# Attention, low-rank mixing and FFN on one core: the early pairs' pooled result goes into the mixing products, and four pairs are early instead of five

## The chip, the cores and the metric

The kernel runs on one core of a Trainium2 chip. The metric is the device time of one execution in microseconds. The core's engines are TensorE (PE; PEld is its weight load), VectorE (DVE), ScalarE (ACT), GpSimd (POOL) and SyncE (SP), each with its own queue of instructions that it works through in order. All DMAs of this kernel are issued by SP.

## The reference, cut to what matters

```python
def _attn_ref(q, k, v):                                # 8 batches, 8 heads, 576 positions, 64 wide
    ...                                                # q_d, k_d, v_d: means over 4 neighbours
    out_d = sm_attn(q_d, k_d, v_d)                     # 144 x 144 attention
    out_up = np.repeat(out_d, factor, axis=2)          # each pooled row four times
    mask = np.abs(pos[:, None] - pos[None, :]) < factor
    ...
    out_local = np.matmul(attn, v)                     # 7 keys around each position
    return (out_up + out_local).astype(np.float32)

def _moe_ref(x, U, V, w_ch1, w_ch2):                   # x: heads side by side, 512 wide
    xt = x.transpose(0, 2, 1)
    h = xt @ U @ V                                     # rank 32, over the positions
    u = x + h.transpose(0, 2, 1)
    ch = np.maximum(u @ w_ch1, 0.0) @ w_ch2            # 512 -> 2048 -> 512
    return (u + ch).astype(np.float32)
```

## The kernel before, in words

Work is cut into 32 pairs of heads, pair = 4 * batch + hp, and 256 FFN steps: batch, one of two halves of 288 positions, and one of 16 slices of 128 hidden channels. A step has a first layer (line 889, tile ps_h, 12 matmuls), ACT and DVE splitting its result into a high and a low part (hH, hL), and a second layer (line 913, tiles acc, 12 matmuls) three steps later. The low parts (W1L, W2L, uL, hL) exist because every FFN product is done three times, high x high, high x low and low x high.

The order on each engine is fixed when the program is built. The code lists operations with an engine, a duration, a priority, tiles read and written; `Plan.run` plays them through, gives out buffers, and writes the instructions in the order of the start times that it found. On the chip each engine follows that order, and waits when something is late.

Before the FFN of a batch can start, its four pairs must have left their mixed result u in the tiles uH and uL, one set for each half. There are two forms of a pair:

- Early form (pairs 0 to 4). The local part is a block product on PE: scores of 32 queries against 38 keys (L602) under a band mask (L613), softmax, transposes (ps_bt, L644) and the product with the values (ps_ba, L656). The pooled part is ps_v, ps_s, ps_t and ps_a (L433 to L486), with the result od. These tiles lie in a memory pool that is given back once all early operations are done; W2's tiles take its place, and the planner's operation "late" stands for that moment. Pairs 0 to 3, which are batch 0, are mixed at once by `early_mix`: hu (L678) multiplies the local result ob by U (Ublk), um (L693, L695) multiplies that (stk) by V and adds ob through the identity. Pair 4 stores its result to DRAM (x_s, L666 and L667), and `mix_part` reads it back later.
- Late form (pairs 5 to 31). Scores of both parts come from PE (L720, L727); the local product is done on POOL (Pt, L800) and DVE (acc, L805) from values vl; the result goes through DRAM (x_s) to `mix_part`: xL, xH and Y, hu (L849), u (L864), then uH on ACT and uL on POOL (L872). There is one vl buffer, and Pt has three buffers, shared with the raw weights w1r and w2r.

In the early form the pooled result reaches the sum in this way: od is stored to DRAM (up_e, L493), and read back (L588) into rows 38 to 45 of each block's value tile vw, after vw's own load:

```python
        for hh in range(2):
            dma(lambda hh=hh: nc.sync.dma_start(
                out=vw_t()[hh * KW + KL:hh * KW + KU, 0:NL],
                in_=up_s()[hh].rearrange("(n j) d -> j n d", j=QL // 4)), [(up_s, hh), (vw_t, hh)], [(vw_t, 2 + hh)], prio, 40)
```

The weight tile ms_b has a fixed pattern in the same eight columns, copied once from pat: a one where the query belongs to that pooled row. So the one product ps_ba adds both parts. vw has two tiles that take turns, so the load of a later pair waits for the ps_ba of an earlier one.

All weights come as 64-bit numbers and are converted in pieces (`convert`): a DMA of 512 KB into a raw buffer, ACT (L346), three DVE operations (L348, L350, L352), ACT for the high part (L354) and POOL for the low one (L357). W1 has 16 pieces and W2 has 16.

## Time and profile before

| | |
|---|---|
| median of 3 runs | 1029.94 us (1028.54 to 1030.81) |
| profiled execution | 1032.15 us |
| its span, first to last instruction | 1030.3 us |
| PE busy | 995.5 us, 97% of the span |
| DVE, ACT, POOL busy | 488.6, 387.3, 539.1 us |
| mean granted clock of PE | 0.978 |
| moved by DMA | 120.30 MB |

A profile is of one execution. Its page has the busy time of each engine, the span in 40 equal slices (digits are tenths), the DMA queues, the chain of work that ended last, followed back from the end, and groups of equal instructions. A row of a timeline has start, duration, engine, line, operation, out<-in, shapes, the count of merged instructions and, in brackets, the idle time of the engine before it with what ended it. One fp32 matmul of the code is two records where its operands are split. A row of waits reads "engine line <- what it waited for: us in total, times, the longest". Busy times of PE overlap, since matmuls are pipelined; the distance from start to start is what one costs in a stream.

### The profile page before, as it was taken

Reading aid. Unit: us, or ns where it says so; the run is one execution under the profiler, and the core shown is the slowest. Engines: PE = TensorE matmul, PEld = TensorE weight load, DVE = VectorE, ACT = ScalarE, POOL = GpSimd, SP = SyncE. Lnnn points to the kernel's source line nnn. Section 1 sums busy time; section 2 is a strip of 40 time slices with the busy share of each in tenths; the row PEclk is TensorE's granted clock in tenths of the full one; section 3 lists DMA queues with packets and bytes.
Section 4 is the critical chain, followed back from the end, with each engine's and each line's share of the span. In section 5 each row is a group of like instructions: output and inputs, shape, how many; then the busy total and the mean of one; then the engine's idle time right before and its main releaser. Section 6 shows DMA issues by size and latency. Waiting matters only on the chain.

```text
span 1030.3 us, 26938 instructions
## 1 busy us (share of the span) xinstructions
PE 995.5 (97%) x10831; PEld 975.6 (95%) x10831; DVE 488.6 (47%) x1018; ACT 387.3 (38%) x1234; POOL 539.1 (52%) x567
## 2 busy tenths in 40 slices
PE   6887899999999999999999999999999999999998
PEld 4666889999999999999999999999999999999998
DVE  5667676555454545445554434553454424212111
ACT  4665565344334433343533235333343232111110
POOL 4643568796755756376775527762675605211010
PEclk9787999999999999999999999999999999999999
DMA  9766874655555444556556336534465231000000
GB/s 292 228 177 181 214 191 126 148 145 131 121 143 117 122 108 100 128 136 145 134 121 137 91 81 146 139 83 113 110 144 131 75 78 35 24 1 24 2 24 24
DMA packets 222612, 120.30 MB, mean 117 GB/s; under 512 B 175492, under 2 KB 198456, under 8 KB 222488
## 3 DMA queue, kind: packets, MB, share of 16 engines
q1 hardware_dynamic: 222488, 118.58, 45.9%
q8 instruction: 85, 1.39, 0.6%
q14 instruction: 39, 0.32, 0.1%
HBM read 87.78 MB, written 30.75 MB: 115 GB/s over the span
## 4 chain that ended last, share of the span: by engine, by line
PE 89%; DMA 5%; ACT 2%; DVE 2%; issue 1%; SPq 1%; DVEq 0%; ACTq 0%
PE acc L913 38%; PE ps_h L889 38%; PE ps_a L554 2%; PE ps_b L720 2%; DMA w2r<-in_W 2%; PE ps_hu L849 2%; PE ps_t L541 1%; PE ps_v L433 1%; PE ps_b L727 1%; PE ps_u L864 1%; PE ps_a L486 1%; DMA vw<-up_e 1%; DMA sc<-s_s 1%; DMA pool_sb<-in_pool 0%; PE ps_hu L678 0%
## 5 line engine op out<-in xcount | busy, mean ns | idle before, releaser
L889 PE MATMUL ps_h<-uH,W1H 128*128 128x288 f32 x1024 | 304.7, 298 | 5.9 <-DVE hL L898 5.9
L913 PE MATMUL acc<-hH,W2H 128*128 128x288 f32 x1024 | 309.7, 302 | 0.0
L889 PE MATMUL ps_h<-uL,W1H 128*128 128x288 f32 x1024 | 303.3, 296 | 0.0
L898 DVE SCALAR_TENSOR_TENSOR hL<-ps_h,hH 128x288 fp32r<-128x288 f32 x256 | 116.6, 455 | 392.3 <-ACT hH L897 391.4
L913 PE MATMUL acc<-hH,W2L 128*128 128x288 f32 x1024 | 302.5, 295 | 0.1
L913 PE MATMUL acc<-hL,W2H 128*128 128x288 f32 x1024 | 302.4, 295 | 0.0
L889 PE MATMUL ps_h<-uH,W1L 128*128 128x288 f32 x1024 | 302.3, 295 | 0.0
L800 POOL TENSOR_TENSOR Pt<-vl,at 128x896 f32<-128x896 f32 (+1 forms) x135 | 233.1, 1815 | 113.0 <-DVE at L783 54.2
L897 ACT ACTIVATE hH<-ps_h 128x288 fp32r<-128x288 f32 x256 | 105.2, 411 | 447.9 <-PE ps_h L889 447.3
L889 PEld LDWEIGHTS ps_h<-uH,W1H 128*128 128x128 f32 x1024 | 193.4, 189 | 7.4 <-DVE hL L898 7.0
L913 PEld LDWEIGHTS acc<-hH,W2H 128*128 128x128 f32 x1024 | 193.1, 189 | 1.1
L889 PEld LDWEIGHTS ps_h<-uH,W1L 128*128 128x128 f32 x1024 | 193.8, 189 | 0.0
L913 PEld LDWEIGHTS acc<-hL,W2H 128*128 128x128 f32 x1024 | 193.4, 189 | 0.0
L913 PEld LDWEIGHTS acc<-hH,W2L 128*128 128x128 f32 x1024 | 193.0, 188 | 0.3 <-POOL W2L L357 0.3
L889 PEld LDWEIGHTS ps_h<-uL,W1H 128*128 128x128 f32 x1024 | 193.3, 189 | 0.0
L805 DVE TENSOR_REDUCE acc<-Pt 128x128 f32<-128x1024 f32 (+1 forms) x135 | 146.0, 1103 | 5.5 <-POOL Pt L800 4.1
L872 POOL TENSOR_TENSOR uL<-xT,uH 128x288 fp32r<-128x288 f32 x56 | 44.1, 812 | 71.4 <-ACT uH L870 70.7
L841 POOL TENSOR_TENSOR xL<-xL,xH 116x640 fp32r<-116x640 f32 x28 | 44.0, 1571 | 69.7 <-ACT xH L840 61.2
L924 POOL TENSOR_TENSOR o<-uH,uL 128x288 f32<-128x288 f32 x64 | 49.7, 816 | 53.0 <-DMA out_t<-o 53.0
L512 POOL TENSOR_TENSOR vr<-vr 72x256 f32<-72x256 f32 x54 | 39.8, 738 | 30.5 <-DMA vr<-in_v 30.1
L794 ACT ACTIVATE Pt<-ul 128x128 f32<-128x128 f32 (+1 forms) x135 | 48.7, 444 | 18.3 <-DVE acc L805 16.0
L745 ACT ACTIVATE se<-ps_b 96x114 f32<-96x114 f32 x108 | 38.6, 357 | 40.7 <-PE ps_b L720 26.7
(130 smaller groups left out, 1046.6 us busy)
## 6 DMA issues: line engine op xcount, KB each, us to landing
vl<-in_vp SPq DMA_DIRECT2D x54, 240.0 KB
out_t<-o SPq DMA_DIRECT2D x64, 144.0 KB
w1r<-in_W SPq DMA_DIRECT2D x16, 512.0 KB
w2r<-in_W SPq DMA_DIRECT2D x16, 512.0 KB
Y<-x_s SPq DMA_DIRECT2D x112, 72.0 KB
gT<-in_kT SPq DMA_DIRECT2D x27, 291.0 KB
xL<-x_s SPq DMA_DIRECT2D x28, 280.0 KB
gq<-in_qT SPq DMA_DIRECT2D x27, 288.0 KB
```

The costliest lines, as they stand in the source:

```text
L512: pool_tt(256, lambda x=x: nc.gpsimd.tensor_tensor(out=x()[:, :, 0:2, :], in0=x()[:, :, 0:2, :], in1=x()[:, :, 2:4, :], op=ALU.add), [x], ...
L745: act(n * KL, lambda p=ps[hh], se=se, n=n, rows=rows: nc.scalar.activation(se()[rows, 0:n].rearrange("p r k -> p (r k)"), p()[rows, 0:n * ...
L794: act(n * D, lambda n=n, ps=ps, Pt=Pt: nc.scalar.activation(Pt()[:, :n, :, 7], ul()[:, ps, :], AF.Copy), [ul], [(Pt, 1)], prio, 0.16)
L800: nc.gpsimd.tensor_tensor(out=Pt()[:, :n, :, 0:7].rearrange("p s d o -> p o s d"), in0=win, in1=at()[:, ps, :].rearrange("p s o -> p o s") ...
L805: dve(8.5 * n * D, lambda n=n, ps=ps, Pt=Pt: nc.vector.tensor_reduce(out=acc()[:, ps, :], in_=Pt()[:, :n], axis=AX.X, op=ALU.add), [(Pt, 0 ...
L841: pool_tt(640, lambda: nc.gpsimd.tensor_tensor(out=xL(), in0=xL().bitcast(F32), in1=xH().bitcast(F32), op=ALU.subtract), [xL, xH], [xL], prio)
L872: pool_tt(TN, lambda uH=uH, uL=uL, uf=uf: nc.gpsimd.tensor_tensor(out=uL()[:, hp, :], in0=uf(), in1=uH()[:, hp, :].bitcast(F32), op=ALU.su ...
L889: nc.tensor.matmul(ps()[:, :TN], w[:, dc, fs], u()[:, dc, :], start=(n == 0), stop=(n == 3 * NDC - 1))
L897: last_h[i] = act(TN, lambda: nc.scalar.activation(hH(), ps()[:, :TN], AF.Relu), [ps], [hH], FIRST, 0.05)
L898: dve(TN, lambda: nc.vector.scalar_tensor_tensor(hL(), ps()[:, :TN], 0.0, hH().bitcast(F32), op0=ALU.max, op1=ALU.subtract), [ps, hH], [hL ...
L913: nc.tensor.matmul(ac[e]()[:, :TN], W2[w][:, fc, es], hx(), start=(fc == 0 and n == 0), stop=(fc == NFC - 1 and n == 2))
L924: pool_tt(TN, lambda e=e, o1=o1: nc.gpsimd.tensor_tensor(out=o1()[:, :TN], in0=uH()[:, e, :].bitcast(F32), in1=uL()[:, e, :].bitcast(F32), ...
```

## The change

The pooled result stays in SBUF. od becomes one of four kept tiles od_e, zeroed once, with the two heads side by side. The stores to up_e, the reloads into vw and the pattern in ms_b are gone; ps_ba works on 38 rows instead of 46. In `early_mix`, hu gets two more products, of od with Upool, which is U summed over four neighbours (made once, by six products and an ACT copy), and um gets one more for each half, of od with a table ex that repeats each pooled row four times. Five pairs in early form become four; pair 4 takes the late form, and the code that stored and held an early pair of batch 1 goes.

```diff
-    NE = 5
+    NE = 4
...
-    pat_sb = early_pool.tile([128, KW - KL], F32, name="pat_sb")
+    ex_sb = early_pool.tile([128, TN], F32, name="ex_sb")
+    Upool = early_pool.tile([128, 2, 2 * R], F32, name="Upool")
...
-    dma(lambda: nc.sync.dma_start(out=pat_sb, in_=pat), [], ["pat"], -5, 14)
...
+        ring([NS, 2, KW], "ms_b", eng=nc.gpsimd)
+    for _ in range(NE):
+        ring([2, 2, D], "od_e", NE, nc.gpsimd)
...
+    nc.gpsimd.memset(Upool, 0.0)
+    dma(lambda: nc.sync.dma_start(out=ex_sb, in_=ex), [], ["ex"], 2.0, 147)
...
+        def u_mm():
+            for n, (r, a) in enumerate(CROSS):
+                nc.tensor.matmul(u4()[:, a], pool_sb[:, 64 - QL * r + QH * a:64 - QL * r + QH * a + QH], Ublk[:, r, 0:R],
+                                 start=(n == 0), stop=(n == len(CROSS) - 1))
+        op(PE, 0.7, u_mm, ["UbH", "pool"], [pu], prio)
+        act(2 * R, lambda: nc.scalar.activation(Upool[:QH, :, 0:R], u4(), AF.Copy), [pu], ["Up"], prio, 0.16)
...
-        od = work(True, glo, [QH, 4, D], F32, "od")
+        od = ring([2, 2, D], "od_e", NE)
...
-        for hh in range(2):
-            dma(lambda hh=hh: nc.sync.dma_start(
-                out=up_s()[hh].rearrange("(a p) d -> p a d", a=2), in_=od()[:, 2 * hh:2 * hh + 2, :]),
-                [(od, hh)], [(up_s, hh)], prio, 40)
+        return od
...
-                    o = slice(hh * KW, hh * KW + KU)
+                    o = slice(hh * KW, hh * KW + KL)
...
-        op(PE, pw(prio) * 2.2, a_mm, [(et, 0), (et, 3)] + [(vw_t, i) for i in range(4)], pa, prio)
+        op(PE, pw(prio) * 2.2, a_mm, [(et, 0), (et, 3)] + [(vw_t, i) for i in range(2)], pa, prio)
...
-                nc.tensor.matmul(ph()[:2 * R, :2 * D], Ublk[:, n, :], flat(n), start=(n == 0), stop=(n == NS - 1))
-        op(PE, pw(prio) * 2.0, hu, rd + ["UbH"], [ph], prio)
+                nc.tensor.matmul(ph()[:2 * R, :2 * D], Ublk[:, n, :], flat(n), start=(n == 0), stop=False)
+            for a in range(2):
+                nc.tensor.matmul(ph()[:2 * R, :2 * D], Upool[:, a, :], up(a), start=False, stop=(a == 1))
+        op(PE, pw(prio) * 2.6, hu, rd + ["UbH", "Up"], [ph], prio)
...
                 nc.tensor.matmul(pu()[:, :TN], stk(), Vst[:, tsl], start=True, stop=False)
+                nc.tensor.matmul(pu()[:, :TN], up(t), ex_sb, start=False, stop=False)
...
-                up_s = buf(dram, [2, SD, D], F32, "up_e", bufs=2)
-                early_global(b, hp, up_s, p, qt, kt, load_vn(b, 2 * hp, p))
-                load_up(vw_t, up_s, p)
-                if b == 0:
-                    x = local_blocks(b, hp, None, qt, kt, vw_t, p + 1)
...
-                else:
-                    x_s = buf(dram, [2, S, D], F32, "x_s", bufs=6)
-                    local_blocks(b, hp, x_s, qt, kt, vw_t, p + 1)
-                    held.append((b, hp, x_s, p + 2))
+                od = early_global(b, hp, p, qt, kt, load_vn(b, 2 * hp, p))
+                x = local_blocks(b, hp, qt, kt, vw_t, p + 1)
...
+                early_mix(b, hp, x, od, p + 2)
```

The changed lists of operations give each engine another order. Three places matter. On SP, in the middle of the W1 loads, before the change:

```order
L392 DMA w1r<-in_W 128x1024
L577 DMA vw_108<-in_vw 48x1152 x2
L510 DMA vr<-in_v 72x2x256
L493 DMA up_e<-od 72x2x64
L577 DMA vw_109<-in_vw 48x1152 x2
L392 DMA w1r<-in_W 128x1024
L588 DMA vw_108<-up_e 8x18x64 x2
L392 DMA w1r<-in_W 128x1024
L493 DMA up_e<-od 72x2x64
L588 DMA vw_109<-up_e 8x18x64
```

and the same place now:

```order
L386 DMA vraw<-in_V 128x576
L509 DMA vr<-in_v 72x2x256
L699 DMA vl<-in_vp 64x960 x2
L394 DMA w1r<-in_W 128x1024 x3
L509 DMA vr<-in_v 72x2x256
L394 DMA w1r<-in_W 128x1024 x2
L509 DMA vr<-in_v 72x2x256
L394 DMA w1r<-in_W 128x1024 x5
L402 DMA w2r<-in_W 128x1024
```

The stores and reloads between the W1 loads are gone, and the loads of vw stand ahead of this piece.

On POOL, around the end of batch 0's FFN (L924 and, in the changed kernel, L914 add uH and uL for its output). Before, the products are those of pair 8, xL is of pair 7, and the five uL are the last one for the first half of batch 1 (pair 7) and all four for its second half:

```order
L872 TENSOR_TENSOR uL<-xT,uH 128x288
L800 TENSOR_TENSOR Pt<-vl,at 128x7x128 x4
L841 TENSOR_TENSOR xL<-xL,xH 116x640
L800 TENSOR_TENSOR Pt<-vl,at 128x7x64
L512 TENSOR_TENSOR vr<-vr 72x2x128
L514 TENSOR_TENSOR vs<-vr 72x128
L924 TENSOR_TENSOR o_3526<-uH,uL 128x288
L924 TENSOR_TENSOR o_3540<-uH,uL 128x288
L924 TENSOR_TENSOR o_3549<-uH,uL 128x288
L924 TENSOR_TENSOR o_3572<-uH,uL 128x288
L872 TENSOR_TENSOR uL<-xT,uH 128x288 x5
```

Now pair 7's products stand just ahead of this piece. The first xL is pair 6's, the products are pair 8's, and the last xL is pair 7's:

```order
L914 TENSOR_TENSOR o_3272<-uH,uL 128x288
L914 TENSOR_TENSOR o_3291<-uH,uL 128x288
L914 TENSOR_TENSOR o_3299<-uH,uL 128x288
L914 TENSOR_TENSOR o_3315<-uH,uL 128x288
L831 TENSOR_TENSOR xL<-xL,xH 116x640
L862 TENSOR_TENSOR uL<-xT,uH 128x288 x2
L511 TENSOR_TENSOR vr<-vr 72x2x128
L513 TENSOR_TENSOR vs<-vr 72x128
L862 TENSOR_TENSOR uL<-xT,uH 128x288 x2
L790 TENSOR_TENSOR Pt<-vl,at 128x7x128 x4
L790 TENSOR_TENSOR Pt<-vl,at 128x7x64
L831 TENSOR_TENSOR xL<-xL,xH 116x640
```

Measured against the output additions of batch 0, the pairs of batch 1 stand one place further back.

On PE, around batch 1's first step. Before, a second layer of batch 0 is followed by batch 1's first first-layer with nothing between, and the mixes of batch 1's first half stand ahead of both:

```order
L913 MATMUL acc_2820<-hH,W2H 128x288
L913 MATMUL acc_2820<-hL,W2H 128x288
L913 MATMUL acc_2820<-hH,W2L 128x288
L889 MATMUL ps_h<-uH,W1H 128x288
L889 MATMUL ps_h<-uL,W1H 128x288
L889 MATMUL ps_h<-uH,W1L 128x288
```

Now, behind batch 0's last second layer, the mixes of pair 6 (its last part) and pair 7 and the values of a later pair stand ahead of batch 1's first step:

```order
L903 MATMUL acc_2525<-hH,W2L 128x288
L854 MATMUL ps_u<-Vst,stk 128x288 x2
L839 MATMUL ps_hu<-xH,Ust 64x128 x5
L839 MATMUL ps_hu<-xL,Ust 64x128 x5
L854 MATMUL ps_u<-Vst,stk 128x288 x2
L553 MATMUL ps_a<-vs,E 72x64 x8
L879 MATMUL ps_h<-uH,W1H 128x288
```

Before, two of batch 0's second layers were still to come when batch 1's first step was issued; now all of them are done ahead of it.

More of the change, by code (lines that the diff above doesn't have):

```diff
@@ L302, in ring @@
             for t in tiles:
-                nc.vector.memset(t[:], 0.0)
+                (eng or nc.vector).memset(t[:], 0.0)
             kept[name] = [0, [Kept(t) for t in tiles]]
-        r = kept[name]
-        r[0] += 1
-        return r[1][(r[0] - 1) % n]
-    def kept_tile(shape, name, n=2):
-        if name not in kept:
-            kept[name] = [0, [Kept(early_pool.tile([128, *shape], F32, name=f"{name}{i}")) for i in range(n)]]
         r = kept[name]
@@ L317, in attn_mix_ffn_kernel @@
     dma(lambda: nc.sync.dma_start(out=eye_sb, in_=eye), [], ["eye"], -5, 33)
-    dma(lambda: nc.sync.dma_start(out=pat_sb, in_=pat), [], ["pat"], -5, 14)
     dma(lambda: nc.sync.dma_start(out=pool_sb, in_=pool), [], ["pool"], 0.05, 74)
-    for _ in range(2):
-        m = kept_tile([NS, 2, KW], "ms_b")
-        op(POOL, 0.4, lambda m=m: nc.gpsimd.tensor_copy(
-            out=m()[:, :, :, KL:KW].rearrange("p r h k -> p (r h) k"),
-            in_=pat_sb.unsqueeze(1).broadcast_to([128, 2 * NS, KW - KL])), ["pat"], [(m, "pat")], 0.1)
     dma(lambda: nc.sync.dma_start(out=ident_sb, in_=ident), [], ["ident"], 0.2, 66)
@@ L584, in load_vn @@
         return t
-    def load_up(vw_t, up_s, prio):
-        for hh in range(2):
-            dma(lambda hh=hh: nc.sync.dma_start(
-                out=vw_t()[hh * KW + KL:hh * KW + KU, 0:NL],
-                in_=up_s()[hh].rearrange("(n j) d -> j n d", j=QL // 4)), [(up_s, hh), (vw_t, hh)], [(vw_t, 2 + hh)], prio, 40)
     def load_kd(b, h0, prio):
@@ L616, in local_blocks @@
         nm, rs = (buf(early_pool, [128, NS, 2], F32, n, None, 2) for n in ("nm", "rs_b"))
-        ms = kept_tile([NS, 2, KW], "ms_b")
+        ms = ring([NS, 2, KW], "ms_b")
         mv = lambda: ms()[:, :, :, 0:KL]
@@ L934, in attn_mix_ffn_kernel, with attention @@
     steps = [(b, t, fc) for b in range(B) for t in range(NT) for fc in range(NFC)]
-    def attention(b, early_part=None):
+    def attention(b):
         for hp in range(HP):
-            if early_part is not None and (b * HP + hp < NE) != early_part:
-                continue
             p = 10.0 * (b * HP + hp)
@@ L966, in attn_mix_ffn_kernel @@
     attention(0)
-    held = []
-    attention(1, True)
     early_ops = list(plan.ops)
@@ L975, in attn_mix_ffn_kernel @@
     load_u(38)
-    for h in held:
-        mix_part(*h)
-    attention(1, False)
+    attention(1)
     for i in range(len(steps) + LAG):
```

44 lines of the change are left out of this document (20 added, 24 removed).

## Prediction

> **What bounds the kernel.** I read the page first, then the span cut at three events, the chain of waits, and the timelines of POOL, DVE, SP and PE there. In the page's slices PE is busy throughout only from the seventh on (each slice is 25.8 us), and its clock is full only from then.
>
> ```profile
> PE   6887899999999999999999999999999999999998
> PEclk9787999999999999999999999999999999999999
> ```
>
> The stretches end at the first FFN matmul (80.4), at the first product of a late pair on POOL (149.6) and at the first FFN matmul of batch 1 (222.6).
>
> ```profile
> 0.00:80.40 80.40, 60.24 (x1024) 50.18 (x1024) 52.24 (x121) 47.99 (x149) 38.01 (x57) 0.85 0.75 225
> 80.40:149.60 69.20, 58.09 (x824) 54.79 (x823) 46.63 (x95) 39.40 (x108) 35.88 (x41) 0.85 0.76 203
> 149.60:222.60 73.00, 72.93 (x765) 72.06 (x766) 46.22 (x92) 36.09 (x122) 60.17 (x56) 1.00 0.60 148
> 222.60:1030.30 807.70, 804.23 (x8225) 798.55 (x8223) 343.48 (x713) 263.84 (x858) 405.06 (x416) 1.00 0.40 96
> ```
>
> The columns are length, then busy time of PE, PEld, DVE, ACT and POOL, then clock, DMA share and GB/s. From 149.6 on PE has no gap worth naming, so whatever the change does there it does by adding PE work or by making a gap. Before that PE loses time, because weights and attention come late. POOL, 60.17 of 73.00 busy in the third stretch, is second in line.
>
> The chain of waits around the start of batch 1 gives the prices of a late pair and the place where it joins:
>
> ```profile
> 168.67 1.03 PE ps_a L554 x16
> 170.16 1.58 PE ps_h L889 x12
> 172.03 0.62 PE ps_b L720 x48
> 172.97 1.80 PE acc L913 x12
> 177.54 0.50 PE ps_t L541 x8
> 216.97 0.60 PE ps_hu L849 x10
> 222.65 1.59 PE ps_h L889 x12
> ```
>
> Scores take 172.97 - (170.16 + 1.58) = 1.23 us, transposes 0.50, values 1.03. The mix of pair 7 starts at 216.97, and batch 1's first FFN step at 222.65. POOL shows why that is just in time:
>
> ```profile
> 149.56 2.01 POOL L800 TENSOR_TENSOR Pt<-vl,at 128x896 f32<-128x896 f32 x1 [0.69 <-DVE c L352]
> 171.31 7.41 POOL L800 TENSOR_TENSOR Pt<-vl,at 128x896 f32<-128x896 f32 x4 [1.79 <-DVE lrl L781]
> 189.85 8.59 POOL L800 TENSOR_TENSOR Pt<-vl,at 128x896 f32<-128x896 f32 x5 [0.80 <-DMA vl<-in_vp]
> 204.51 7.37 POOL L800 TENSOR_TENSOR Pt<-vl,at 128x896 f32<-128x896 f32 x4
> 220.40 0.80 POOL L872 TENSOR_TENSOR uL<-xT,uH 128x288 fp32r<-128x288 f32 x1 [1.46 <-ACT uH L870]
> ```
>
> The products of pairs 5, 6, 7 and 8 start at 149.56, 171.31, 189.85 and 204.51. The last tile of pair 7 is ready at 220.40 + 0.80 = 221.2, and PE takes it at 222.65: 1.45 us of slack. Call 149.56 T0. It is set by the weights: POOL waits there for the third DVE operation of the fifteenth W2 conversion, since products and raw weights share three buffers.
>
> ```profile
> 88.70 0.67 DVE L352 SCALAR_TENSOR_TENSOR c<-w2r,y_h 128x512 int32<-128x512 int32 x1
> 148.80 0.68 DVE L352 SCALAR_TENSOR_TENSOR c<-w2r,y_h 128x512 int32<-128x512 int32 x1
> DVE y_h L348 <- ACT c L346: 10.4, 6, 3.3
> DVE uL L701 <- ACT uH L699: 4.2, 2, 4.0
> DVE xT L839 <- DMA Y<-x_s: 3.0, 1, 3.0
> DVE y_h L348 <- ACT ob L660: 2.2, 1, 2.2
> ```
>
> The first two are the first and the fifteenth of 16 such operations, 60.1 us apart. The other four are DVE's waits from 60 to 156, in us, times and the longest.
>
> **The change, part by part.**
>
> *The DRAM trip goes.* Twenty DMAs of 36 KB leave SP's queue. For pair 3:
>
> ```profile
> 57.49 0.29 SPq L493 DMA_DIRECT2D up_e<-od  x1
> 62.53 0.32 SPq L588 DMA_DIRECT2D vw<-up_e  x1
> 78.44 0.33 SPq L493 DMA_DIRECT2D up_e<-od  x1
> 79.07 0.33 SPq L392 DMA_DIRECT2D w1r<-in_W  x1
> SPq L493 <- DVE od L489: 16.0, 7, 10.2
> 62.53 5.92 DMA vw<-up_e
> ```
>
> The store goes out at 57.49, the reload at 62.53, and the data is there, for the local product (ps_ba), at 62.53 + 5.92 = 68.45: 11 us in series. Worse, SP stood 10.2 us at a store of pair 4, up to 78.44, with the last W1 load (79.07) and all W2 loads queued behind it. Now ps_ba needs no pooled result and runs two to three places earlier. The late reads that follow are the mix's own: od straight from SBUF.
>
> The Trainium skill, "DMA: Bandwidth & Descriptors", section "Anatomy of one DMA", puts a DMA at a fixed 2.0 us plus bytes over 436 GB/s, fitted on another issue path; an estimate from it is 2.1 us each, 4.2 for the trip. The trace has 5.0 and 5.9, so by the page the trip would be worth 7 us less; the sum takes the trace.
>
> *Added PE passes in the early mix.* Each of four pairs gets two 128-column products in hu and two 288-column products in um; once, six 32-column products make Upool.
>
> ```profile
> 46.45 1.31 PE L678 MATMUL ps_hu<-ob,Ublk 128*64 128x128 f32 x10
> 49.09 0.75 PE L695 MATMUL ps_u<-ident_sb,ob 128*128 128x128 f32 x6
> 49.67 0.38 PE L693 MATMUL ps_u<-Vst,stk 128*128 128x288 f32 x1
> 70.73 1.32 PE L695 MATMUL ps_u<-ident_sb,ob 128*128 128x128 f32 x6
> ```
>
> Five hu products take 1.31 us, so two take 0.5. Three identity products cover 288 columns in 49.67 - 49.09 = 0.58, at the lower clock up to 1.32 with their drain. So 4 x (0.5 + 2 x 0.58) = 6.6, and Upool about 0.5 by its columns (a quarter of a ps_v pass, below): 7.1 us, at the lower clock 13.
>
> *Pair 4 leaves the early stage.* Its scores, ps_v, ps_s, transposes, half its values (0.7) and its ps_ba go:
>
> ```profile
> 59.21 1.53 PE L433 MATMUL ps_v<-vn,pool_sb 128*72 128x128 f32 x12 [0.19 <-DVE uL L701]
> 71.87 1.71 PE L644 MATMUL ps_bt<-ident_sb,ms_b 128*128 128x128 f32 x5
> 92.10 1.41 PE L656 MATMUL ps_ba<-vw,et 46*32 46x64 f32 x80
> ```
>
> That is 4.65 us here, and with the smaller ones about 8. PE's early work thus falls by about 1 us, or grows by 5 if much of it runs at the lower clock. It is not what shortens the stage. Also gone are pair 4's loads, its x_s stores, its held mix on DVE (the 3.0 and 2.2 us waits are its), and 3 us of DVE work. POOL's seven new memsets, near 3 us by their columns, stand ahead of its first pooling, which waits for data anyway; the two copies of the pattern go. The ex table is one more DMA of 144 KB behind the first W1 load: 0.5 us of transfer ahead of pair 1's loads, taken as nothing because three dependent copies went.
>
> *T0 moves.* The first FFN step follows the last early mix. Pair 3's ps_s stood here:
>
> ```profile
> 42.91 1.25 PE L446 MATMUL ps_s<-smk,smq 64*72 64x144 f32 x8
> 50.00:70.00 20.00, 15.02 (x336) 12.38 (x335) 16.37 (x33) 15.43 (x45) 11.55 (x13) 0.92 0.77 210
> ```
>
> In the new PE order three ps_ba, three ps_bt and a hu stand ahead of it, where before there were waits; I leave it at 44. What remains by the prices above is four um of 2 x (0.38 + 2 x 0.58) = 3.1 us, three hu of 1.8, and about 4 us of ps_ba, ps_bt, transposes and values: some 22 us, and 4 us of waits for stk. So 44 + 26, with 2 for the clock, makes 72 instead of 80.4. The first W2 conversion came 9.6 us after the last W1 load (79.07 to 88.70); of the 10.2 us hole ahead of that load I count 6.7, since the raw buffers then set the pace: near 82 instead of 88.70. The stretch to the fifteenth then loses the waits of pair 4 (2.2 and 3.0), the wait in which three converted W2 tiles sat behind pair 5's score load, and its share of the DMA-late 10.4: about 42 instead of 60.1. T0 near 82 + 42.5 = 124.5, 25 earlier, where the 42 is my estimate and the softest number here. Ends: only the waits named for pair 4, the 4.2 and 3 us of work gone, 12.4: 137. DVE does 52.24 + 46.63 = 98.9 us of work up to T0; 96 of it at 16.37 of 20, the share it held from 50 to 70, gives 117. I take 124.5, between, since the SP hole and the hold-ups of pair 4 are separate.
>
> *Batch 1 now needs four late pairs.* Pairs 4 to 7 go through POOL one after another, and in POOL's order pair 8's products stand ahead of pair 7's mix, as before. So from T0 to batch 1's first step there is one more cycle: 73.1 (222.65 - 149.56) plus 18.5 (171.31 to 189.85) or 14.7 (189.85 to 204.51); I take 17.5: 90.6. Batch 0's FFN ends before that: its last second-layer step stands behind the mix of pair 6, and from that mix to batch 1's first step there are 17.5 + 5.7 (216.97 to 222.65) = 23.2 us, with 4.1 of PE work in them (that step 1.6, two mixes, one values pass). So a PE gap of 19 us is on the path. Batch 1 starts at 124.5 + 90.6 = 215.1 instead of 222.65: -7.5.
>
> *After it.* Of the added pair, scores and transposes (1.23 + 0.50) lie behind that point: +1.7. After the stall the clock must recover:
>
> ```profile
> 100.00:110.00 10.00, 10.00 (x69) 9.99 (x62) 5.57 (x14) 7.62 (x19) 5.80 (x6) 0.79 0.80 166
> ```
>
> That slice follows PE gaps: PE is busy for all of it, at a clock of 0.79, so 10 x 0.21 = 2.1 us are lost: +2.1.
>
> Sum: -7.5 + 1.7 + 2.1 = -3.7. The profiled execution took 1032.15 around a span of 1030.3; the median of the runs is 1029.94, 2.2 lower. Against the median: 1026.
>
> **Rivals.**
>
> *It cancels.* T0 moves by 21.3 (19 to 23), and gain and stall meet: 1028 to 1032. For it: DMA was 0.76 busy in the second stretch, and with conversions denser the three raw buffers wait for loads of 512 KB, the 10.4 us growing.
>
> *The new wait wins (slower).* One mechanism: the pair moved to the late form costs a POOL cycle at batch 1's start and nothing returns it. It decides when T0 is later than 128.25 (where 128.25 + 90.6 + 3.8 = 222.65). With T0 at 131 to 137 the time is 1032.7 to 1038.7; with 18.5 for the cycle 1039.7. For it: the early mix grew by 7 to 13 us on the very PE that must open the FFN, and the waits named for the removed work are only 12.4. Against it: SP's 10.2 us hole, in which no weight was fetched.
>
> The Trainium skill, "TensorE: Matmul & The Clock Gate", Part 1, also speaks against the change: after an idle window of about 3.4 us the clock halves, and it takes about as long to come back. By the page the restart costs 3.4 x 0.5 = 1.7 where I have 2.1; the sum would be 0.4 lower.
>
> *No stall at batch 1.* POOL had 12.8 us idle in the third stretch; if pair 4's products started while W2 still loads, the extra cycle would vanish and PE's own work would decide: 1026 - 19 - 2.1, about 1005. Against it: the buffers that products need are the raw weights'.
>
> *Nothing happens early* (the round trip was hidden, T0 stays near 149): 1051. Against it are pair 4's removed waits. I leave it 2 in 100.
>
> **Chances.** Forecast 0.48 (1016 to 1028), cancels 0.17, slower 0.30 with 0.02 more for nothing early, no stall 0.03. A change under 0.2%, 2 us, cannot be told from none. Faster 0.51, same 0.17, slower 0.32. The range for 8 in 10 runs from 117 + 87.8 - 222.65 + 3.8 = -14.05 (1016) to the 1039 of the slower case; the forecast's own is 1016 to 1028.
>
> **What would show it.** Right: no up_e DMA; DVE's fifteenth W2 operation and POOL's first product near 124 (117 to 131); first FFN matmul near 72; PE gaps of 12 to 22 us in all just before batch 1, released by the mix of pair 7, its clock below full; batch 1 near 215; from there to the end 811.5 (807.7 + 3.8). Wrong if T0 falls outside 117 to 137, if the POOL cycle is not 15 to 18, or if later batches stall too.

## The result, and the profile after

The change made the kernel slower: 1044.89 us (1044.12 to 1045.9) against 1029.24 (1027.12 to 1030.81), a ratio of 1.0137 with a 95% interval of 1.0115 to 1.0159. The forecast was 1026, its range 1016 to 1039.

The span of the changed kernel, cut at the same three events as before (first FFN matmul, first late-pair product on POOL, first FFN matmul of batch 1), with the same columns (length, busy time of PE, PEld, DVE, ACT and POOL, clock, DMA share, GB/s):

```profile
0.00:78.74 78.74, 59.87 (x953) 51.09 (x953) 48.62 (x110) 43.32 (x130) 36.52 (x56) 0.87 0.65 205
78.74:144.15 65.41, 56.91 (x764) 52.95 (x763) 48.38 (x100) 42.09 (x122) 34.34 (x40) 0.95 0.76 213
144.15:234.90 90.75, 76.06 (x779) 74.36 (x778) 55.49 (x101) 35.63 (x111) 74.54 (x71) 0.93 0.54 134
234.90:1043.00 808.10, 804.55 (x8305) 798.52 (x8304) 345.51 (x712) 268.73 (x877) 404.30 (x415) 1.00 0.41 97
```

The sum is made in these rows. T0 moved from 149.56 to 144.15: -5.4. From T0 to batch 1's first step it takes 90.75 instead of 73.09: +17.7. From there to the end 808.10 instead of 807.65: +0.45. Together +12.7, which is 1043.0 against 1030.3. (By medians the change costs 15.7; the profiled execution before was 2.9 above its median.) Executions of one kernel differ by several us, 1026.5 to 1034.2 for the kernel before beside experiment 1, and each trace is of one of them, so a T0 that differs by 3 us between two kernels shows little by itself.

POOL's products of pairs 4 to 8, and PE just before batch 1, in the timelines of the changed kernel; the last row is of the chain of waits:

```profile
144.15 2.03 POOL L790 TENSOR_TENSOR Pt<-vl,at 128x896 f32<-128x896 f32 x1 [0.32 <-DVE ri L531]
165.61 7.42 POOL L790 TENSOR_TENSOR Pt<-vl,at 128x896 f32<-128x896 f32 x4 [2.12 <-DMA vl<-in_vp]
184.10 8.48 POOL L790 TENSOR_TENSOR Pt<-vl,at 128x896 f32<-128x896 f32 x5
201.02 8.39 POOL L790 TENSOR_TENSOR Pt<-vl,at 128x896 f32<-128x896 f32 x5
220.61 7.72 POOL L790 TENSOR_TENSOR Pt<-vl,at 128x896 f32<-128x896 f32 x5
...
226.72 0.80 PE L839 MATMUL ps_hu<-xH,Ust 116*64 116x128 f32 x5 [9.07 <-ACT xH L830]
229.81 0.80 PE L839 MATMUL ps_hu<-xL,Ust 116*64 116x128 f32 x5 [2.29 <-POOL xL L831]
...
234.90 2.99 PE ps_h L879 x12
```

There is the forecast's gap: PE waits for the mix of pair 7, which on POOL stands behind the products of pair 8 (220.61). The third stretch has 90.75 - 76.06 = 14.7 us of it, and batch 1's first step runs at half speed, 2.99 us instead of 1.59. What is not there is the early T0. The conversions on DVE (the third W1 piece, the first and the fifteenth W2 piece) show it:

```profile
32.55 0.67 DVE L345 SCALAR_TENSOR_TENSOR c<-w1r,y_a 128x512 int32<-128x512 int32 x1
90.41 0.68 DVE L345 SCALAR_TENSOR_TENSOR c<-w2r,y_h 128x512 int32<-128x512 int32 x1
143.43 0.64 DVE L345 SCALAR_TENSOR_TENSOR c<-w2r,y_h 128x512 int32<-128x512 int32 x1
```

The third W1 piece came 7 us later than before (its row before: 25.56), the first W2 piece 1.7 later, and the fifteenth 5.4 earlier. PE shows what happened between 18 and 31 us, the changed kernel first (with the waits of ACT and DVE there), then the kernel before:

```profile
18.02 0.57 PE L649 MATMUL ps_ba<-vw,et 38*32 38x64 f32 x35
21.15 0.81 PE L649 MATMUL ps_ba<-vw,et 38*32 38x64 f32 x45 [2.56 <-issue]
22.38 1.58 PE L370 MATMUL ps_p<-Ublk,pool_sb 128*72 128x32 f32 x12
27.48 1.64 PE L665 MATMUL ps_hu<-ob,Ublk 128*64 128x128 f32 x10
30.17 1.03 PE L448 MATMUL ps_s<-smk,smq 64*72 64x144 f32 x8
52.46 1.16 PE L448 MATMUL ps_s<-smk,smq 64*72 64x144 f32 x8
...
22.01 0.44 ACT L653 ACTIVATE ob<-ps_ba 128x320 f32<-128x320 f32 x1 [4.76 <-PE ps_ba L649]
25.01 0.29 DVE L491 TENSOR_TENSOR od_e<-ps_a,ri 72x128 f32<-72x128 f32 x1 [6.01 <-PE ps_a L488]
```

```profile
21.46 1.25 PE L446 MATMUL ps_s<-smk,smq 64*72 64x144 f32 x8
25.56 0.69 DVE L352 SCALAR_TENSOR_TENSOR c<-w1r,y_a 128x512 int32<-128x512 int32 x1
```

Since ps_ba no longer waits for DRAM, the planner put pair 0's local product, with Upool (ps_p) and hu, ahead of the scores of pair 1 (ps_s). Those came at 30.17 instead of 21.46; 2.56 us of that are a pause of PE inside ps_ba that the last section comes back to. ACT, whose copy of ps_ba stood ahead, waited 4.76 us, DVE 6.01, and behind them, in order, came the W1 conversions and the next softmax. Pair 3's scores came at 52.46 instead of 42.91.

The change did gain something here. The twelfth and thirteenth W1 pieces, the changed kernel first, then the kernel before:

```profile
74.31 0.68 DVE L345 SCALAR_TENSOR_TENSOR c<-w1r,y_a 128x512 int32<-128x512 int32 x1
77.46 0.69 DVE L345 SCALAR_TENSOR_TENSOR c<-w1r,y_a 128x512 int32<-128x512 int32 x1
```

```profile
67.18 0.69 DVE L352 SCALAR_TENSOR_TENSOR c<-w1r,y_a 128x512 int32<-128x512 int32 x1
78.33 0.67 DVE L352 SCALAR_TENSOR_TENSOR c<-w1r,y_a 128x512 int32<-128x512 int32 x1
```

Up to the twelfth piece the change is 7.1 us behind. Between the two pieces the kernel before takes 11.2 us and the changed kernel 3.2. So the change gained 8.0 us there, and the early order had nearly used them up. What part of the 8.0 is the trip's is not shown.

### The profile page after: what moved, and what is told of

Read it like the earlier page. It is cut to its first block, busy times and chain, and to the rows that moved or that the text cites. A ratio compares the mean times of both kernels' runs of the same rounds, so it can differ in the third digit from the quotient of the medians.

```text
span 1043.0 us, 26873 instructions
## 1 busy us (share of the span) xinstructions
PE 997.4 (96%) x10792; PEld 976.9 (94%) x10792; DVE 498.0 (48%) x1022; ACT 389.8 (37%) x1239; POOL 549.7 (53%) x580
## 4 chain that ended last, share of the span: by engine, by line
PE 77%; POOL 1%; DVE 0%; issue 0%; ACT 0%; POOLq 0%; DVEq 0%
PE acc L903 35%; PE ps_h L879 34%; PE ps_a L553 2%; PE ps_b L710 2%; PE ps_hu L839 1%; PE ps_t L540 1%; PE ps_b L717 1%; POOL Pt L790 1%; PE ps_u L854 1%; DVE o L917 0%; POOL xL L831 0%; POOL uL L862 0%; DVE xT L857 0%; ACT uH L860 0%; DVE stk L844 0%
## 5 line engine op out<-in xcount | busy, mean ns | idle before, releaser
L790 POOL TENSOR_TENSOR Pt<-vl,at 128x896 f32<-128x896 f32 (+1 forms) x140 | 240.4, 1805 | 108.6 <-DVE acc L795 44.6
L879 PEld LDWEIGHTS ps_h<-uH,W1H 128*128 128x128 f32 x1024 | 193.7, 189 | 11.2 <-DVE hL L888 10.9
L795 DVE TENSOR_REDUCE acc<-Pt 128x128 f32<-128x1024 f32 (+1 forms) x140 | 151.3, 1104 | 11.1 <-POOL Pt L790 8.9
L862 POOL TENSOR_TENSOR uL<-xT,uH 128x288 fp32r<-128x288 f32 x56 | 44.2, 815 | 80.4 <-ACT uH L860 80.1
L831 POOL TENSOR_TENSOR xL<-xL,xH 116x640 fp32r<-116x640 f32 x28 | 44.0, 1572 | 74.4 <-ACT xH L830 68.5
L914 POOL TENSOR_TENSOR o<-uH,uL 128x288 f32<-128x288 f32 x64 | 49.8, 819 | 53.0 <-DMA out_t<-o 53.0
```

The source lines that it names most:

```text
L790: nc.gpsimd.tensor_tensor(out=Pt()[:, :n, :, 0:7].rearrange("p s d o -> p o s d"), in0=win, in1=at()[:, ps, :].rearrange("p s o -> p o s") ...
L795: dve(8.5 * n * D, lambda n=n, ps=ps, Pt=Pt: nc.vector.tensor_reduce(out=acc()[:, ps, :], in_=Pt()[:, :n], axis=AX.X, op=ALU.add), [(Pt, 0 ...
L831: pool_tt(640, lambda: nc.gpsimd.tensor_tensor(out=xL(), in0=xL().bitcast(F32), in1=xH().bitcast(F32), op=ALU.subtract), [xL, xH], [xL], prio)
L862: pool_tt(TN, lambda uH=uH, uL=uL, uf=uf: nc.gpsimd.tensor_tensor(out=uL()[:, hp, :], in0=uf(), in1=uH()[:, hp, :].bitcast(F32), op=ALU.su ...
L879: nc.tensor.matmul(ps()[:, :TN], w[:, dc, fs], u()[:, dc, :], start=(n == 0), stop=(n == 3 * NDC - 1))
L914: pool_tt(TN, lambda e=e, o1=o1: nc.gpsimd.tensor_tensor(out=o1()[:, :TN], in0=uH()[:, e, :].bitcast(F32), in1=uL()[:, e, :].bitcast(F32), ...
```

## The experiments

Ratios are against runs of the kernel before on the same chip, with 95% intervals. T0 is always the first late-pair product on POOL.

**1. Only four early pairs.** The DRAM trip stays.

```diff
-    NE = 5
+    NE = 4
```

> The kernel before with four early pairs instead of five and nothing else: the pooled result still goes through DRAM. T0 is the start of the first late-pair product on POOL (149.56 before, 144.15 in the changed kernel); from T0 to batch 1's first step there were 73.1 us before and 90.7 in the changed kernel. Theory 'one more POOL cycle': those 90 us come from the pair count alone, and nearly all of the 5.4 us of T0 too, since pair 4's work is what left the early stage; then T0 is 142 to 147, batch 1 starts at 232 to 238, time 1040 to 1048. Rival 'the trip': the 5.4 us of T0 come from the removed DRAM trip; then T0 stays at 149 to 151 here and the time is 1048 to 1052. Rival 'the added passes': the trip's removal gained more than 5.4, and PE passes ate it; then T0 is 149 or later here as well, or, if the passes ate more than the trip gave, T0 is 135 to 141 and the time 1032 to 1039.

Measured: 1041.42 us, ratio 1.0103 (1.0065 to 1.0141). The product row of POOL and the chain's row of batch 1's first steps (24 matmuls, two steps):

```profile
146.13 2.02 POOL L800 TENSOR_TENSOR Pt<-vl,at 128x896 f32<-128x896 f32 x1 [2.10 <-DVE c L352]
...
234.66 4.20 PE ps_h L889 x24
```

T0 is 3.4 earlier than in the trace of before, and batch 1 came 88.5 after it instead of 73.1. So the pair count alone makes most of the loss, as the theory of one more POOL cycle says; "the trip" and "the added passes" both missed the time.

**2. Only the mixing.** Five early pairs; pairs 0 to 3 mixed as in the change, pair 4 with its pooled result through DRAM and the pattern columns.

```diff
-    NE = 4
+    NE = 5
...
-                od = early_global(b, hp, p, qt, kt, load_vn(b, 2 * hp, p))
+                up_s = buf(dram, [2, SD, D], F32, "up_e", bufs=1) if b else None
+                od = early_global(b, hp, p, qt, kt, load_vn(b, 2 * hp, p), up_s)
```

> The changed kernel's mixing for batch 0 (pairs 0 to 3), but five early pairs: pair 4 keeps the early form, with its pooled result through DRAM and the pattern columns, as before. Theory 'one more POOL cycle': from T0 to batch 1 there are 71 to 76 us again, no PE gap before batch 1; T0 is 146 to 152, since pair 4's early work is back; time 1025 to 1033. Rival 'the trip': T0 keeps its 5.4 us, 143 to 145, time 1022 to 1026. Rival 'the added passes': the early mix makes T0 later than before, 154 to 160, and the time 1034 to 1041, above the kernel before.

Measured: 1035.22 us, ratio 1.0040 (1.0023 to 1.0057). With the order that the planner gave it, the mixing is slower than the trip. Only the rival of the added passes had this time, but its T0 (154 to 160) did not come: T0 is 148.29, where the theory had it. The trace loses its time behind T0. Batch 1 starts 76.9 us later instead of 73.1; PE was busy for 73.36 of them, and the largest wait, 2.2 us in two pieces, was for the hL of its own FFN steps. No wait names POOL's products. The two parts add up: 1.0103 and 1.0040 make 1.0143, and the change has 1.0137.

**3. and 4. What paces the W2 pieces.** Both are the changed kernel in unchanged order. In one the second DVE operation of a W2 piece is left out, in the other half of each load (the conversion then uses the loaded half twice).

```diff
-        dve(1.15 * n, lambda: nc.vector.scalar_tensor_tensor(
+        dve(1.15 * n, (lambda: None) if name == "c2" else lambda: nc.vector.scalar_tensor_tensor(
```

```diff
...
-        dma(lambda: nc.sync.dma_start(out=raw(), in_=w2.bitcast(I32)[f * 128:(f + 1) * 128, :]),
+        dma(lambda: nc.sync.dma_start(out=raw()[:, :CN], in_=w2.bitcast(I32)[f * 128:(f + 1) * 128, :CN]),
```

> The changed kernel without the second of the three DVE operations of each W2 conversion (16 of 0.69 us, 11 us of DVE work; the sign of W2 is left out of the computation). Order unchanged. Theory 'DVE paces the W2 conversions': the stretch from the first to the fifteenth (53.0 us) shrinks by 7 to 11, T0 134 to 138, and the time falls by as much, 1034 to 1038. Rival 'the loads pace them': the waits of ACT for w2r (11.3 us) grow instead, T0 moves by 0 to 2, time 1043 to 1046.

> The changed kernel with half of each W2 load (256 KB instead of 512; half the columns are loaded and used twice, so the second layer's weights are not the reference's). Instructions and order unchanged. Rival 'the loads pace the W2 conversions': ACT's waits for w2r (11.3 us) nearly vanish, the stretch of 53.0 us shrinks by 5 to 10, T0 134 to 139, time 1034 to 1040. Theory 'DVE paces them': T0 moves by 0 to 2, time 1043 to 1046. If both this and the run with less DVE work gain 3 to 5, the two alternate.

Measured: 1047.63 us, ratio 1.0164 (1.0133 to 1.0195), with less DVE work; 1039.87, ratio 1.0084 (1.0054 to 1.0113), with half loads. The waits of ACT for the raw weights between 60 and 144 (to 148 in the second) in the changed kernel, with less DVE work, and with half loads:

```profile
ACT c L339 <- DMA w2r<-in_W: 11.3, 8, 4.0
```

```profile
ACT c L339 <- DMA w2r<-in_W: 12.4, 9, 4.2
```

```profile
ACT c L343 <- DMA w2r<-in_W: 5.4, 6, 3.0
```

Taking 11 us of DVE work away moved T0 not earlier but 3.5 later (147.6); why later is open. Halving the loads moved T0 to 137.56, by 6.6 (this execution was 2.1 below its median; by the medians the time fell by 5.0). The stretch from the first to the fifteenth piece fell from 53.0 to 48.6 (88.21 to 136.85). So the loads pace a part of it, about 4 us, and DVE's busy time does not; the sum's end of 117, which let DVE set the pace, is not borne out. Batch 1 started 90.4 after T0 with half loads too, as in the changed kernel.

**5. A second vl buffer, first form.** In the changed kernel a pair's values vl can be loaded only when the products of the pair before have let go of the one buffer. Room for a second comes from the output tiles.

```diff
-        vl = lb([128, NPOS + 6, D], "vl")
+        vl = lb([128, NPOS + 6, D], "vl", None, 2)
...
-                if e == NDC - 1:
-                    o1 = buf(loc, [128, TN], F32, "o1", "o1b", 1)
-                else:
-                    o1 = buf(ffn, [128, CN], F32, "o1", "cT:o1", 3)
+                o1 = buf(ffn, [128, CN], F32, "o1", "cT:o1", 3)
```

> The changed kernel with two vl buffers instead of one (room for it comes from the fourth output tile, which now shares the ring of the other three). In the changed kernel POOL's products of pairs 4 to 8 start at 144.15, 165.61, 184.10, 201.02 and 220.61 and are busy 7.4 to 8.5 us each; between them POOL waits for the next vl, whose load can start only when the products have let go of the one buffer. Theory 'the added POOL cycle is the price of the fourth late pair, and a cycle is products plus reload': the products now follow one another in 10 to 13 us, batch 1 starts 12 to 20 earlier (214 to 222), and the time is 1026 to 1034, with the early stage as it was (T0 142 to 147). Rival 'the cycle is set by the whole chain to the mix, not by vl': batch 1 starts at 229 to 235 as before, time 1040 to 1045.

Measured: 1050.80 us, ratio 1.0184 (1.0162 to 1.0205): a miss. Batch 1 did start about 79 us after T0, but T0 was 149.33, and the rest took some 14 us longer. The edit holds two things, the second buffer and the output tiles; experiment 6 has the first without the second.

**6. The same with room from elsewhere.** Two vl buffers, one buffer for the score copies instead of two.

```diff
-            se = buf(loc, [128, LB, KL], F32, "se", bufs=2)
+            se = buf(loc, [128, LB, KL], F32, "se", bufs=1)
```

> The changed kernel with two vl buffers; the room comes from the score copies (se) with one buffer instead of two, and the output tiles stay as they are. With the shared output ring the same edit brought batch 1's start from 90.5 to 79.2 us after T0, but T0 to 149.3 and the rest from 808 to 822 us. Theory 'a POOL cycle is products plus vl reload, and the output ring cost the rest': batch 1 starts 76 to 82 after T0, T0 143 to 150, rest 805 to 811, time 1028 to 1038. Rival 'a second vl buffer costs the stream itself': rest again above 815, time 1040 to 1052.

Measured: 1032.18 us, ratio 1.0011 (0.9988 to 1.0034). Windows from T0 to batch 1 and to the end, and the chain's row:

```profile
147.69:222.12 74.43, 71.85 (x746) 69.95 (x745) 50.52 (x91) 32.94 (x104) 67.01 (x60) 1.00 0.55 137
222.12:1033.10 810.98, 807.43 (x8329) 801.63 (x8327) 350.08 (x724) 272.75 (x890) 411.50 (x425) 1.00 0.41 98
```

```profile
222.12 4.71 PE ps_h L879 x24
```

74.4 us instead of 90.75 with the same four late pairs, although T0 is 3.5 later (in an execution 2.7 above its median). The last product of pair 7, and then POOL's two longest waits from 144 to 235 in the changed kernel:

```profile
197.84 1.07 POOL L790 TENSOR_TENSOR Pt<-vl,at 128x448 f32<-128x448 f32 x1
```

```profile
POOL uL L862 <- ACT uH L860: 10.7, 4, 4.1
POOL Pt L790 <- DMA vl<-in_vp: 2.1, 1, 2.1
```

The products of pairs 4 to 7 are done 51.2 us after T0, where the changed kernel needs 65.3 (201.02 + 8.39 - 144.15): 14.1 of the 16.3 us. So a second vl buffer shortens the cycles, and with it nearly all of the loss is gone. How it does so is less sure. POOL itself waited only 2.1 us for vl in the changed kernel and 10.7 for uH; with one buffer the products of a pair stand in the plan behind the reload, and other work, with waits of its own, stands between. With two buffers the whole plan is another one (pair 7's xL now stands ahead of four of the five products of pair 8), and no run takes the reload away without changing the order.

**7. Order held back, four pairs.** The changed kernel; ps_ba of a pair waits in the plan for ps_s two places on, hu for ps_s three places on. `score_op` and `hold_op` collect these operations as they are planned.

```diff
+    for p, o in hold_op:                 # ps_ba: p = pair + 2, hu: p = pair + 3
+        d = score_op[min(p, NE - 1)]
+        if o not in d.succ:
+            d.succ.append(o)
+            o.ndep += 1
     early_ops = list(plan.ops)
```

> The changed kernel with the local product of an early pair (ps_ba) held back behind the pooled scores (ps_s) of the pair two places on, and its hu behind those three places on: about the places that they had before the change. Computation and instruction counts are the same, the order differs. In the changed kernel ps_ba, u_mm and hu of pair 0 stand ahead of ps_s of pair 1, which came at 30.17 instead of 21.46, and the third W1 conversion at 32.55 instead of 25.56. Theory 'the early order delayed the weights': ps_s of pair 1 is back at 21 to 23, the W1 and W2 conversions come 4 to 8 earlier, T0 136 to 140, time 1036 to 1041. Rival 'what was lost early is made up by the conversions later': T0 142 to 147, time 1042 to 1046.

Measured: 1034.91 us, ratio 1.0048 (1.0025 to 1.0071), 9 to 10 us less than the change. PE's scores of pair 1, the first product on POOL, and the chain's row of batch 1's first step:

```profile
22.16 1.25 PE L449 MATMUL ps_s<-smk,smq 64*72 64x144 f32 x8
```

```profile
137.95 2.00 POOL L791 TENSOR_TENSOR Pt<-vl,at 128x896 f32<-128x896 f32 x1 [1.12 <-DVE c L346]
```

```profile
224.68 2.68 PE ps_h L880 x12
```

T0 is 6.2 earlier, waiting again for the fifteenth piece, and batch 1 comes 86.7 after it instead of 90.75 (the order on POOL changed with the plan). Nothing was computed less. The first W2 piece came at 85.87 instead of 90.41, and the stretch from there to the fifteenth took 51.3 instead of 53.0. The early order cost the change 6 us of T0, and some 4 of the cycle came with it.

**8. Order held back, five pairs.** The same edit in the kernel of experiment 2.

> The kernel with five early pairs and the new mixing for pairs 0 to 3 (1035.2, 3.4 above the kernel before beside it), with ps_ba and hu held back in the same way. Theory 'the early order costs those 3.4': 1028 to 1032, no slower than the kernel before, PE less idle from 80 to 160. Rival 'the passes cost them': 1034 to 1037. Rival 'the planner's later order does' (a W2 piece that waits behind another pair's scores): between or above, 1031 to 1040, with the idle time of PE in another place.

Measured: 1030.51 us, ratio 0.9997 (0.9976 to 1.0018): experiment 2's loss is gone, by the order alone. With about its old order the mixing takes as long as the trip, within the interval. But the gain did not come by T0. The first product on POOL and the chain's row of batch 1's first step:

```profile
149.03 2.06 POOL L816 TENSOR_TENSOR Pt<-vl,at 128x896 f32<-128x896 f32 x1 [1.55 <-DVE c L348]
```

```profile
219.73 1.58 PE ps_h L905 x12
```

The scores of pair 1 are back at 22.13 (28.70 in experiment 2), yet the first FFN step came at 88.36 instead of 76.42 and T0 at 149.03 instead of 148.29. What got shorter is the way from T0 to batch 1, 70.7 instead of 76.9 us, in which PE waited 0.5 us. With five early pairs the order costs time, but not by the path that experiment 7 shows for four.

**9. Without the added passes.** In three kernels, the order unchanged; the same edit each time.

```diff
-                nc.tensor.matmul(ph()[:2 * R, :2 * D], Ublk[:, n, :], flat(n), start=(n == 0), stop=False)
-            for a in range(2):
-                nc.tensor.matmul(ph()[:2 * R, :2 * D], Upool[:, a, :], up(a), start=False, stop=(a == 1))
+                nc.tensor.matmul(ph()[:2 * R, :2 * D], Ublk[:, n, :], flat(n), start=(n == 0), stop=(n == NS - 1))
...
-                nc.tensor.matmul(pu()[:, :TN], up(t), ex_sb, start=False, stop=False)
...
-            for n, (r, a) in enumerate(CROSS):
+            for n, (r, a) in enumerate(CROSS[2:4]):
```

> The same kernel with five early pairs, order unchanged, without the added passes (the two products of hu and the one of each um are left out, and four of the six that make Upool; batch 0's pooled part is missing from the result). Theory 'the passes cost the 3.4': PE's early work falls by 7 to 8 us, first FFN step at 69 to 72 instead of 76.4, time 1027 to 1032. Rival 'the order does': the first FFN step comes earlier by 3 to 7, but the W2 pieces do not, and the time is 1033 to 1036.

> Four early pairs, new mixing held back (1034.9), order unchanged, without the added passes. Theory 'the passes are on the path to T0': T0 133 to 136 instead of 137.95, time 1030 to 1033. Rival 'T0 follows the weights, which the passes do not hold': T0 137 to 139, time 1034 to 1036.

> Five early pairs, new mixing held back, two vl buffers (1029.7; the kernel before with two vl buffers and the DRAM trip has 1024.2), order unchanged, without the added passes (batch 0's pooled part is missing from the result). Theory 'the passes cost PE time ahead of the FFN, and it is on the path': first FFN step 5 to 8 earlier than 87.05, batch 1 at 212 to 215, time 1022 to 1026. Rival 'the gap of 5.5 is the order that the planner made': time 1028 to 1031.

Measured, in the kernel of experiment 2: 1031.43 us, ratio 1.0005 (0.9988 to 1.0022), 3.8 less. But its profiled execution, the slowest of the ten (4.6 above the median), shows the first FFN step at 77.3, no earlier than 76.4, and T0 later, so it does not show where the time went. In the kernel of experiment 7: 1030.85, ratio 0.9999 (0.9982 to 1.0017), 4.1 less, and here the first product shows it:

```profile
134.55 2.03 POOL L788 TENSOR_TENSOR Pt<-vl,at 128x896 f32<-128x896 f32 x1 [1.12 <-DVE c L346]
```

T0 is 3.4 earlier than 137.95, with both profiled executions within 0.5 us of their medians; batch 1 starts 86.9 after it, as without the edit. So about half of the 7.1 us of passes lies on the path to T0 in this kernel. In the kernel of experiment 11 below: 1028.90, ratio 0.9966 (0.9945 to 0.9987), only 0.8 less, a miss, although its profile has the first FFN step 4.5 earlier and T0 3.2 earlier; of the 3.1 us between the two profiled executions, 2.3 come from where they lie in their groups (one 1.3 above its median, the other 1.1 below).

**10. Order held back and two vl buffers, four pairs.**

> Both: four early pairs and the new mixing, ps_ba and hu held back to their old places (1034.9 by itself, T0 137.95, batch 1 at 224.4), and two vl buffers with one se buffer. If T0 stays at 136 to 142 and the products of four late pairs take 76 to 82 us to batch 1's first step, that step stands at 214 to 222 and the time is 1022 to 1031, the best so far. If one se buffer or the second vl delays the W2 conversions instead, T0 is above 145 and the time 1033 to 1042.

Measured: 1032.06 us, ratio 1.0003 (0.9980 to 1.0026): a miss, no better than experiment 6. T0 is 141.08 instead of the 137.95 of experiment 7 (in an execution 2.9 above its median), and it is 82 us from there to batch 1 instead of the 74.4 of experiment 6: the two gains do not add up. Why the cycle is longer again is open.

**11. The same, five pairs; and the kernel before with two vl buffers, with five and with four early pairs.**

> Five early pairs, the new mixing for batch 0 with ps_ba and hu held back (1030.5 by itself, as before the change), and two vl buffers with one se buffer. PE had no gap before batch 1 in the run without the second buffer, so POOL's cycle is not what it waits for: expected 1028 to 1033. Rival 'POOL's cycle holds PE here too': 1022 to 1027.

> The kernel before with two vl buffers and one se buffer and nothing else: what the second buffer is worth without the change. PE has no gap from 150 us on there, so: same, 1028 to 1034. Rival 'earlier products of late pairs take POOL and DMA time from the W2 pieces': 1034 to 1042.

> The kernel before with four early pairs and two vl buffers (with five and two: 1024.2; with four and one: 1041.4). Theory 'the price of the fourth late pair is the vl reload in POOL's cycle': most of the 10.6 us is gone, 1024 to 1031. Rival 'four late pairs do not fit ahead of batch 1 in any case': 1034 to 1040, with a PE gap before batch 1's first step.

Measured: 1029.71 us, ratio 0.9978 (0.9962 to 0.9993), with the mixing; 1024.20, ratio 0.9936 (0.9914 to 0.9958), for the kernel before with two vl buffers, the best of all and better than both; 1026.47, ratio 0.9949 (0.9929 to 0.9969), for the same with four early pairs. The last says that four late pairs do fit, at a price of about 2 us instead of 10.6, with two vl buffers. But not by the cycle alone: against experiment 1, T0 came at 135.40 instead of 146.13, batch 1 80.1 us after it instead of 88.5, and the rest took 6.3 longer. So a plan with a second vl buffer moved T0 by 10.7 us, with the scores of pair 1 where they had been (21.27 and 21.52). The early order, worth 6 us in the changed kernel, is not the only thing that sets T0. The run before, with five early pairs, was forecast as "same", wrongly. Its first product, and what SP waited for at the pooled stores from 60 to 160:

```profile
142.62 2.05 POOL L800 TENSOR_TENSOR Pt<-vl,at 128x896 f32<-128x896 f32 x1 [0.89 <-DVE c L352]
```

```profile
SPq L493 <- DVE od L489: 2.7, 2, 1.9
```

T0 came 6.9 earlier, with the trip in place. In that stretch SP waited 2.7 us at these stores instead of 11.6 (longest 1.9 instead of 10.2), since the new plan put them elsewhere. That the hole which I read in SP's queue is worth about 7 us fits this, but the run changes more than that, so it is not shown. The run does show that the hole needs no new mixing to go.

## Why the prediction was wrong, point by point

- **From T0 to batch 1: right.** Forecast 90.6, measured 90.75. The PE gap was to be 19 us (12 to 22) and is 14.7, in the place and behind the mix that were named. That the sum came within 0.2 us is luck: its 17.5 was picked between 14.7 and 18.5, and the cycles of the changed kernel are 21.5, 18.5, 16.9 and 19.6. And "one POOL cycle" hid the cost of a single vl buffer, which experiment 6 takes away; the rows of vl stood in the trace of before (the 0.80 us wait for vl at 189.85) and were not used.
- **T0: wrong, and it decides.** Forecast 124.5 (117 to 137), measured 144.15, outside its ends. Of the 19.65 us, 8.4 are the first W2 piece (90.41 instead of 82) and 11.2 the way from it to the first product (53.7 instead of 42.5). The step that failed first is "Pair 3's ps_s stood here ... I leave it at 44". It came at 52.46. From there to the first FFN step the working holds: 26 us and 2 for the clock were forecast, and 52.46 to 78.74 is 26.3. The order that I quoted, "three ps_ba, three ps_bt and a hu stand ahead of it, where before there were waits", was read as free filling. But ps_s is the head of the chain of every pair, and what stands ahead of it delayed DVE, ACT and the weights behind it. Experiment 7 shows the cost in this kernel: 6.2 us of T0, with ps_s of pair 3 at 47.45, still not at 44. Experiment 8 gives back the 3.4 us of experiment 2 by the order too, but behind T0.
- **The passes:** summed at 7.1 us and then cancelled against pair 4's work ("not what shortens the stage"). Experiment 9 puts 3.4 us of them on the path to T0 in the four-pair kernel.
- **The W2 stretch, the larger part of the miss, is a mis-sized term:** "about 42 instead of 60.1" for the first to the fifteenth W2 piece. It measured 53.0 in the change, 51.3 with the order held back, and 48.9 without the passes as well (84.89 to 133.80, in the kernel of experiment 7). There T0 is 134.55, 15.0 earlier than before instead of 25; of the 10 us that are left, 7 are this stretch and 3 its start. The waits of pair 4 went, but ACT's wait for raw weights, which I had falling, stayed (11.3 us, 10.0 in the kernel before). With half loads (experiment 4) it is 5.4 and the stretch 48.6, so the loads explain a part. What keeps the stretch from 42 is open; no run reached it.
- **SP's hole of 10.2 us** did go. The W1 pieces were then late for another reason: the third came 7.0 us later and the first W2 piece 1.7 later, instead of 6.7 earlier. The 8.0 us that the change gained between the twelfth and the thirteenth W1 piece are near the 6.7, but they need not be the hole's: in the kernel before, the load of the thirteenth had been issued ahead of the hole (three loads from 63.19 to 68.27).
- **After batch 1's start:** forecast +3.8, measured +0.45. The clock cost about 2.5 us there (below), near the 2.1 counted. What the sum left out was in the quoted order: two second layers of batch 0, 1.6 us each, stood behind batch 1's start before and stand ahead of it now, where PE had to wait anyway. With them, 1.7 + 2.5 - 3.2 makes 1.0.
- **The rival that came true** is "the new wait wins", with a chance of 0.30. Its rule gives the time: 144.15 + 90.6 + 3.8 - 222.65 = 15.9, so 1045.8 against 1044.89. Its T0 was bounded at 137 because I took the removed waits as gone whatever the order. A bound for T0 should also have held the case in which PE's new order holds the scores back: with the 8.5 us by which pair 3's ps_s missed its 44, the end of 137 would have stood at 145.5, and the time at 1047.
- **A reading of the page:** PE's digits are 9 from the sixth slice on and its clock's from the fifth, not from the seventh. Nothing in the sum rests on it.

## What to carry to other kernels

When a change takes a wait away from an operation, look where the scheduler then puts it: work that became ready early was put ahead of the head of another chain, and in the changed kernel that order cost 6 us of T0 without a single instruction more. Before pricing a cycle of an engine by its distance from start to start, split it into work and waits, and ask which buffer holds the next work back; here a second buffer was worth more than either form of the change. And a queue's hole is worth its length only if the loads behind it have nothing else to be late for.

## What the runs showed of the hardware

Within the 80 small matmuls of ps_ba PE stood still with nothing in the profile that released it, 2.56 and 1.11 us in the change. With the order held back (experiment 7) it came there as well, later:

```profile
38.05 0.67 PE L650 MATMUL ps_ba<-vw,et 38*32 38x64 f32 x29 [3.92 <-issue]
```

No such row stands in the first 100 us of the kernel before. It is not bound to the new form, though: in experiment 1, which has the old one, 3.25 us of it stand before 71.12. What PE waits for there is open; no run took it away.

After the gap the clock came back slowly. Windows of the changed kernel, 4 us each:

```profile
228.00:232.00 4.00, 1.23 (x7) 1.05 (x7) 2.15 (x5) 0.54 (x2) 3.92 (x6) 0.50 0.55 146
232.00:236.00 4.00, 3.69 (x23) 3.34 (x23) 1.24 (x3) 0.81 (x2) 3.81 (x6) 0.50 0.29 94
236.00:240.00 4.00, 4.00 (x106) 3.56 (x106) 0.46 (x1) 0.56 (x2) 4.00 (x4) 0.52 0.37 74
240.00:244.00 4.00, 4.00 (x32) 4.00 (x31) 1.28 (x3) 3.38 (x16) 1.00 (x2) 1.00 0.79 152
```

PE was busy for 7.69 of the 8 us from 232 to 240, at about half clock. That is some 4 us lost, about 1.5 of them ahead of batch 1's first step and 2.5 behind it. The Trainium skill, "TensorE: Matmul & The Clock Gate", Part 1, has full clock return after about 3.4 us of sustained work; here it took about twice that.
